# A fused attention, expert and gated kernel: the gated stage in blocks of 512 tokens, with the last 64 tokens of all batches as one unit

## The chip, the cores and the metric

One NeuronCore of a Trainium2 chip runs the whole kernel. The metric is the device time of one execution in microseconds (us). TensorE is clocked at one of two levels, 1.2 or 2.4 GHz; the profile gives the granted share of the upper one.

## The reference

Three layers follow each other. The first is an attention over 32 memory slots for each of 8 heads; the second gives each token one of 8 experts (two products with a ReLU between, scaled by a probability p); the third, the one that changes here, is a gated convolution along the tokens. S = 576 tokens, B = 4 batches, model width 512, inner width 1024:

```python
h = np.maximum(x @ w_in, 0.0)                     # [4, 576, 1024]
hp = zero-padded h, one token on each side
conv_out = sum(conv_w[k] * hp[:, k:k + 576] for k in range(3))
gate = 1.0 / (1.0 + np.exp(-conv_out))
out = (h * gate) @ w_out                          # [4, 576, 512]
```

Everything is float32. The kernel gets that precision from a faster type by writing each operand as a high and a low part and adding three products (high with high, high with low, low with high).

## The kernel before

The attention and the experts run batch by batch, with a product order written out by hand. An expert stage leaves its output `y` (not yet times p) in the DRAM buffer `ydram`, in 8 stores of 288 tokens for each batch, issued by GpSimd (POOL). The last product of batch 3 is followed on TensorE by the gated stage, the function `gated`, with no gap in the program.

The gated stage holds the inner dimension on the partitions, in 8 blocks of 128 (`f`), and tokens along the free axis. For each batch `b` it loads `y` and the row p (`load_y`, `load_p`), multiplies them and splits the product into `yh` and `yl` (`split_y`). Then, for each `f`:

- TensorE adds 12 terms (4 pieces of the model width, 3 products each) into the PSUM tile `pi`. A bank holds 512 float32 columns, so the 576 tokens stand as two halves of 288 in two banks (`banks`, two such pairs): 24 products of 288 columns.
- ScalarE (ACT) takes the ReLU out of PSUM into `ht` and multiplies by the middle tap into `ct`. VectorE (DVE) adds the two other taps (two operations), ScalarE takes the sigmoid, VectorE multiplies (`gm`), ScalarE and VectorE split the result into the tile `g` (`gs`; for f = 3, 4 and 6 the subtraction is GpSimd's). `ht` and `ct` come from one ring of 6 buffers (tag `cv`), so three blocks can be under way.
- GpSimd copies the last 64 tokens of `g` into `tail`, which holds two batches side by side.

After the 8 blocks, TensorE multiplies by `w_out` in chunks of 128 tokens (`po`, 24 products of 512 columns each): four chunks for each batch, and after an odd batch a fifth for the 64-token tails of two batches. That makes 18 chunks. The buffers of `y` (tag `ay`) are two in all, shared with the attention's last operand.

The order on TensorE is that of the program in the expert stage and in batch 0 of the columns (`tc.keep_in_program_order`); elsewhere a scheduler of the compiler lays the instructions of every engine in order when the program is built, and each engine then works its list strictly in that order, waiting on semaphores. SyncE (SP) issues the loads, in its own order.

```python
matmul3([(ps[:, hf, :HALF], half(hf)) for hf in range(2)],
        [((wi[kc][:, 0, fs], wi[kc][:, 1, fs]), (yh[:, kc, :], yl[:, kc, :])) for kc in range(4)],
        tc.keep_in_program_order if b == 0 else lambda ins: ins)
```

Of the kernel before, what the change touches and what calls it, by code (L numbers as in the profile page):

```python
# [24 lines left out]
HALF = S // 2  # L25
EPS = 1e-9
# [90 lines left out]
def fused_kernel(tc, q, first, first_q, kv, kv_tail, phi, w1, w2, w_in, conv_w, w_out, out):  # L117
# [3 lines left out]
    with (  # L121
# [779 lines left out]
        def load_p(name, e, b):  # L901

            p = late[1].tile([128, S], F32, tag="p", bufs=2, name=f"p{name}")
            nc.sync.dma_start(p, pdram[ds(e + 8 * b, 1), :].to_broadcast([128, S]))
# [16 lines left out]
        def y_parts(b):  # L921
            return [late[1].tile([128, 4, S], F32R, tag=t, bufs=1, name=f"{t}{b}") for t in ("yh", "yl")]
# [100 lines left out]
        def gated(gp, nm, scaled=False):  # L1023
# [9 lines left out]
            tail = None  # L1033
            for b in range(B):
                yh, yl = ys
                gs = []
                if b + 1 < B:
                    yn = load_y(b + 1, first(b + 1))
                if b % 2 == 0:
                    tail = gp.tile([128, 8, 2, 128], F32R, tag="tail", bufs=1, name=f"tail{b}")  # L1040
                to = 64 * (b % 2)
                def gate(f, ht, ct):
                    nc.scalar.activation(ct, ct, AF.Sigmoid)  # L1043
                    slow(f"gm.{f}").tensor_tensor(ct, ht, ct, ALU.mult)  # L1044
                    t = gp.tile([128, 2, S], F32R, tag="g", name=f"g{nm}{b}_{f}")

                    def finish():
                        split(t[:, 0, :], t[:, 1, :], ct, slow(f"gs.{f}"))
                        nc.gpsimd.tensor_copy(tail[:, f, :, to:to + 64], t[:, :, 512:576].bitcast(F32))  # L1049

                    gs.append(t)
                    return finish

                before = None
                for f in range(8):
                    fs = slice(f * 128, (f + 1) * 128)
                    ps = banks(f"pi{b}_{f}")
                    matmul3([(ps[:, hf, :HALF], half(hf)) for hf in range(2)],
                            [((wi[kc][:, 0, fs], wi[kc][:, 1, fs]), (yh[:, kc, :], yl[:, kc, :])) for kc in range(4)],
                            tc.keep_in_program_order if b == 0 else lambda ins: ins)  # L1060
                    finish = gate(*before) if before else lambda: None
                    ht = lp.tile([128, S], F32, tag="cv", name=f"ht{b}_{f}")
                    nc.scalar.activation(two(ht), halves(ps), AF.Relu)  # L1063
                    ct = lp.tile([128, S], F32, tag="cv", name=f"ct{b}_{f}")
                    nc.scalar.activation(ct, ht, AF.Copy, scale=convw[:, 1, f:f + 1])  # L1065
                    nc.vector.scalar_tensor_tensor(  # L1066
                        ct[:, 1:], ht[:, :S - 1], convw[:, 0, f:f + 1], ct[:, 1:], ALU.mult, ALU.add)
                    nc.vector.scalar_tensor_tensor(  # L1068
                        ct[:, :S - 1], ht[:, 1:], convw[:, 2, f:f + 1], ct[:, :S - 1], ALU.mult, ALU.add)
                    finish()  # L1070
                    before = f, ht, ct
                    while len(wo) < 4 and f >= WO[len(wo)]:
                        wo.append(w2_piece(f"wo{len(wo)}", slow(f"wo.{len(wo)}")))
                gate(*before)()
# [4 lines left out]
                def product(ps, c, fr, cols=slice(0, 512)):  # L1079
# [104 lines left out]
```

## Time and profile before

| | us |
|---|---|
| three timed runs | 411.52, 411.10, 409.93; median 411.1 |
| the profiled execution, its time | 411.57 |
| the profiled execution, its span | 409.8 |
| TensorE busy | 402.3 (98% of the span) |
| VectorE, ScalarE, GpSimd busy | 276.0, 221.8, 75.0 |

The span runs from the first to the last recorded instruction, so 1.8 us of the execution's time lie around it. Times in the rows are counted from the start of the span. The gated stage fills its second half, from 205.6 on. In a row, "x" is a count, and the square bracket tells how long the engine was idle before the row and who ended that. "PEld" is TensorE's weight load, which overlaps its products; busy times of overlapping products can't be added up.

### The profile page before, as it was taken

To read this page: it belongs to the slowest core of one execution; us is meant where nothing else is said; L and a number is where in the kernel's file an instruction comes from. 1 tells how busy PE (TensorE), PEld (TensorE's weight loads), DVE (VectorE), ACT (ScalarE), POOL (GpSimd) and SP (SyncE) were. 2 spreads that over 40 slices of the span, in tenths; PEclk is the share of its full clock that TensorE was granted. 3 is DMA by queue.
4 is the path that set the end of the run, shared out by engine and by line. 5 is a ranking of instruction groups with operands and counts; after the bars stand their busy time and mean duration, and the time that the engine had idled before them with its cause. 6 is when DMAs were issued, how large, how long until landed. Compare 5 with 4: busy or idle time off the path is not lost. (4 is left out here: it accounts for less than half of the span.)

```text
span 409.8 us, 8399 instructions
## 1 busy us (share of the span) xinstructions
PE 402.3 (98%) x3350; PEld 369.3 (90%) x3351; DVE 276.0 (67%) x505; ACT 221.8 (54%) x420; POOL 75.0 (18%) x125
## 2 busy tenths in 40 slices
PE   7999999999999999999999999999999999999996
PEld 6769989899998998999999988998889998999884
DVE  2689798897787986696879981679204793077700
ACT  4457567564566456465857652677215772267411
POOL 1000101402122211310101620033200233004400
PEclk9999999999999999999999999999999999999999
DMA  7999989999484959947550032000020000200022
GB/s 269 334 391 408 353 262 316 386 416 412 116 298 161 360 182 387 385 157 199 184 162 2 0 117 102 2 0 2 23 81 26 2 0 2 102 2 0 2 81 56
DMA packets 23888, 69.04 MB, mean 168 GB/s; under 512 B 3264, under 2 KB 4032, under 8 KB 23840
## 3 DMA queue, kind: packets, MB, share of 16 engines
q1 hardware_dynamic: 20256, 56.88, 39.2%
q0 software_dynamic: 3584, 11.54, 7.2%
q8 instruction: 28, 0.46, 0.5%
q14 instruction: 20, 0.16, 0.1%
HBM read 52.08 MB, written 16.33 MB: 167 GB/s over the span
## 5 line engine op out<-in xcount | busy, mean ns | idle before, releaser
L166 PE MATMUL py<-h,wb 128*128 128x288 f32 x768 | 105.3, 296 | 0.2 <-DVE h L807 0.2
L166 PEld LDWEIGHTS py<-h,wb 128*128 128x128 f32 x768 | 102.3, 188 | 1.2 <-issue 0.4
L166 PE MATMUL pi<-yh,wi 128*128 128x288 f32 x512 | 91.0, 296 | 0.0
L1084 PE MATMUL po<-wo,g 128*128 128x512 f32 x360 | 84.2, 389 | 0.0
L1084 PEld LDWEIGHTS po<-wo,g 128*128 128x128 f32 x360 | 67.0, 188 | 13.1
L166 PEld LDWEIGHTS pi<-yh,wi 128*128 128x128 f32 x512 | 76.6, 189 | 1.1 <-ACT ht L1063 0.2
L1066 DVE SCALAR_TENSOR_TENSOR ct<-ht,convw,ct 128x575 f32<-128x575 f32 x32 | 31.0, 968 | 51.2 <-ACT ct L1065 51.2
L166 PE MATMUL pi<-yl,wi 128*128 128x288 f32 x256 | 54.7, 295 | 0.0
L166 PE MATMUL ph<-att,vh 128*128 128x288 f32 x256 | 53.2, 301 | 0.2 <-DVE h L807 0.2
L1049 POOL CAST tail<-g 128x128 fp32r<-128x128 f32 x32 | 23.0, 722 | 123.2 <-DVE g L154 122.6
L891 POOL DMA_DIRECT2D ydram<-ys x32 | 17.6, 549 | 144.8 <-ACT ys L890 126.2
L166 PEld LDWEIGHTS ph<-att,vh 128*128 128x128 f32 x256 | 40.5, 188 | 3.7 <-DVE h L807 1.5
L166 PEld LDWEIGHTS pi<-yl,wi 128*128 128x128 f32 x256 | 41.1, 188 | 0.0
L1063 ACT ACTIVATE ht<-pi 128x576 f32<-128x576 f32 x32 | 20.8, 649 | 32.7 <-PE pi L166 32.7
L166 PE MATMUL ph<-att,vl 128*128 128x288 f32 x128 | 37.5, 294 | 0.0
L807 DVE SCALAR_TENSOR_TENSOR h<-ph,h 128x288 fp32r<-128x288 f32 x64 | 27.7, 449 | 12.1 <-ACT h L806 11.9
L806 ACT ACTIVATE h<-ph 128x288 fp32r<-128x288 f32 x64 | 25.4, 409 | 18.2 <-PE ph L166 18.0
L1110 ACT ACTIVATE ot<-po 128x512 f32<-128x512 f32 x17 | 9.5, 598 | 42.1 <-PE po L1084 42.1
L1044 DVE TENSOR_TENSOR ct<-ht,ct 128x576 f32<-128x576 f32 x32 | 27.0, 845 | 7.3 <-ACT ct L1043 7.1
L890 ACT ACTIVATE ys<-py 128x288 f32<-128x288 f32 x32 | 13.1, 408 | 33.9 <-issue 18.4
L153 ACT ACTIVATE g<-ct 128x576 fp32r<-128x576 f32 x32 | 21.7, 680 | 13.0 <-DVE ct L1044 13.0
L1068 DVE SCALAR_TENSOR_TENSOR ct<-ht,convw,ct 128x575 f32<-128x575 f32 x32 | 28.4, 886 | 0.4
(231 smaller groups left out, 513.0 us busy)
## 6 DMA issues: line engine op xcount, KB each, us to landing
kv<-in_kv SPq DMA_DIRECT2D x14, 512.0 KB, 8.3
q<-in_q SPq DMA_DIRECT2D x8, 576.0 KB, 10.1
ydram<-ys POOLq DMA_DIRECT2D x32, 144.0 KB, 5.3
y<-ydram SPq DMA_DIRECT2D x4, 1152.0 KB, 6.5
out<-ot SPq DMA_DIRECT2D x15, 256.0 KB, 2.1
ph<-in_phi SPq DMA_DIRECT2D x8, 288.0 KB, 7.4
adram<-at POOLq DMA_DIRECT2D x8, 288.0 KB, 7.2
wa_1r<-in_w SPq DMA_DIRECT2D x4, 512.0 KB, 5.5
```

The source lines that it names most:

```text
L153: pin(nc.scalar.activation(hi, src, AF.Copy))
L166: pin(nc.tensor.matmul(ps, st, mv[:, cols], start=i == 0, stop=i == len(terms) - 1))
L806: nc.scalar.activation(t[:, 0, :], ps, AF.Relu)
L807: low = nc.vector.scalar_tensor_tensor(t[:, 1, :], ps, 0.0, t[:, 0, :].bitcast(F32), ALU.max, ALU.subtract)
L890: nc.scalar.activation(yt, ps, AF.Copy)
L891: stored.append(nc.gpsimd.dma_start(ydram[b, d, :, half(hf)], yt).ins)
L1044: slow(f"gm.{f}").tensor_tensor(ct, ht, ct, ALU.mult)
L1049: nc.gpsimd.tensor_copy(tail[:, f, :, to:to + 64], t[:, :, 512:576].bitcast(F32))
L1063: nc.scalar.activation(two(ht), halves(ps), AF.Relu)
L1066: nc.vector.scalar_tensor_tensor(ct[:, 1:], ht[:, :S - 1], convw[:, 0, f:f + 1], ct[:, 1:], ALU.mult, ALU.add)
L1068: nc.vector.scalar_tensor_tensor(ct[:, :S - 1], ht[:, 1:], convw[:, 2, f:f + 1], ct[:, :S - 1], ALU.mult, ALU.add)
L1084: last_product[:] = [nc.tensor.matmul(ps[:, cols], st[sp], w[:, mp, f % 2, cols], start=f == 0 and i == 0, stop=f == 7 and i == 2).ins]
```

## The change

Each batch's first 512 tokens are one product of 512 columns for each term and block (`MT`), in a single bank; four such banks stand in a pool of their own. Of its 512 columns 511 outputs are finished there, since token 511's convolution needs token 512. The last 66 tokens of every batch (`TW`; 64 of them new, two as neighbours) are loaded, scaled and split together (`load_tails`, `split_tails`), and make one unit of 4 x 66 = 264 columns, worked once between batch 0 and the products by `w_out`. It gives the 64 tail tokens of all batches and token 511 (`edge`), which GpSimd copies into each `g` (`close_main`). So `pi` has 4 x 96 products of 512 columns and 96 of 264, where it had 768 of 288. The products by `w_out` keep their number and shape; for the last batch their order is now the written one. The loads of `y` bring 512 tokens; eight small loads bring the tails. The convolution for the middle tap moves into `taps`. Apart from that, the keys and values of units 4 to 6 of the attention are loaded by one DMA where it was two.

```diff
+MT, TW = 512, 66
...
-                if u < 2 * B - 1:
+                if u < 4:
                     for i in range(2):
...
-            nc.sync.dma_start(y, ydram[b].rearrange("d p s -> p d s"))
-            return y, load_p(b, e, b) if e is not None else None
+            nc.sync.dma_start(y[:, :, :MT], ydram[b].rearrange("d p s -> p d s")[:, :, :MT])
+            return y[:, :, :MT], load_p(b, e, b, MT)[:, :MT] if e is not None else None
...
+        def load_tails(scaled):
+
+            y = state.tile([128, 4, S], F32, tag="ay", name="yt")[:, :, :B * TW]
+            p = None if scaled else late[1].tile([128, S], F32, tag="p", bufs=2, name="pt")[:, :B * TW]
+            for b in range(B):
+                if not scaled:
+                    nc.sync.dma_start(by_batch(p)[:, b], pdram[ds(expert(b) + 8 * b, 1), S - TW:].to_broadcast([128, TW]))
+                nc.sync.dma_start(y[:, :, TW * b:TW * b + TW], ydram[b].rearrange("d p s -> p d s")[:, :, S - TW:])
+            return y, p
+
+        def split_tails(yp, nm):
+            y, p = yp
+            t = state.tile([128, 2, 4, B * TW], F32R, tag="ay", name=f"ts{nm}")
+            parts = [t[:, i] for i in range(2)]
+            if p is not None:
+                nc.vector.tensor_tensor(y, y, p.rearrange("p (o s) -> p o s", o=1).to_broadcast([128, 4, B * TW]), ALU.mult)
+            split(*parts, y)
+            return parts
...
+            def taps(ct, ht, f, n, first):
+
+                w = lambda k: convw[:, k, f:f + 1]
+                more = min(n, ht.shape[-1] - first - 1)
+                nc.scalar.activation(ct, ht[..., first:first + n], AF.Copy, scale=w(1))
+                a = 1 - first
+                nc.vector.scalar_tensor_tensor(ct[..., a:], ht[..., :n - a], w(0), ct[..., a:], ALU.mult, ALU.add)
+                nc.vector.scalar_tensor_tensor(ct[..., :more], ht[..., first + 1:first + 1 + more], w(2), ct[..., :more],
+                                               ALU.mult, ALU.add)
+
+            def columns(name, y, store, pin=lambda ins: ins, between=lambda f: None):
...
-                    ps = banks(f"pi{b}_{f}")
-                    matmul3([(ps[:, hf, :HALF], half(hf)) for hf in range(2)],
...
+                    ps = pairs[-1].tile([128, 512], F32, tag="pi", bufs=1 if scaled else 4, name=f"pi{name}_{f}")[:, :n]
+                    matmul3([(ps, slice(0, n))],
+                            [((wi[kc][:, 0, fs], wi[kc][:, 1, fs]), (yh[:, kc, :], yl[:, kc, :])) for kc in range(4)], pin)
...
+            def store_tail(f, ct):
+                hi, lo = (by_batch(tail[:, f, i]) for i in range(2))
+                split(hi, lo, ct[:, :, 1:], slow(f"gs.{f}"))
+                split(edge[:, f, 0], edge[:, f, 1], ct[:, :, 0])
...
+                def close_main(f):
+                    nc.gpsimd.tensor_copy(gs[f][:, :, MT - 1:], edge[:, f, :, b:b + 1].bitcast(F32))
...
+                columns(f"{nm}{b}", ys, store_main, tc.keep_in_program_order if b == 0 else lambda ins: ins, between)
+                if b == 0:
+                    tails = split_tails(tails, nm)
+                    yn = load_y(1, first(1))
+                    columns(f"{nm}t", tails, store_tail)
+                    for f in range(8):
+                        close_main(f)
...
+                pin = tc.keep_in_program_order if b == B - 1 else lambda ins: ins
...
+        ps2_cm.__exit__(None, None, None)
+        pi_cm = tc.tile_pool(name="ps3", bufs=4, space=PSUM)
```

On TensorE, at the end of batch 0's columns (the number after `pi0_` is the block f; a row is a run of equal instructions). Before, the last block and then `po`:

```order
L166 MATMUL pi0_7_3346<-yh0_2931,wi3_2976 128x288 x2
L166 MATMUL pi0_7_3346<-yl0_2932,wi3_2976 128x288 x2
L166 MATMUL pi0_7_3346<-yh0_2931,wi3_2976 128x288 x2
L1084 MATMUL po0_0_3403<-wo0_3186,g0_1_3168 128x512 x2
L1084 MATMUL po0_0_3403<-wo1_3263,g0_2_3216 128x512 x3
```

Now the tails' blocks `pit` stand there, the first three ahead of any product by `w_out`:

```order
L168 MATMUL pi0_7_3264<-yh0_2928,wi3_2973 128x512
L168 MATMUL pi0_7_3264<-yl0_2929,wi3_2973 128x512
L168 MATMUL pi0_7_3264<-yh0_2928,wi3_2973 128x512
L168 MATMUL pit_0_3301<-ts_3293,wi0_2814 128x264 x3
...
L168 MATMUL pit_2_3345<-ts_3293,wi0_2814 128x264 x3
L168 MATMUL pit_2_3345<-ts_3293,wi1_2817 128x264 x3
L168 MATMUL pit_2_3345<-ts_3293,wi2_2970 128x264 x3
L168 MATMUL pit_2_3345<-ts_3293,wi3_2973 128x264 x3
L1146 MATMUL po0_0_3523<-wo0_3156,g0_0_3121 128x512 x3
```

The 24 products of a block became 12, and `pit_0` to `pit_2` come before the first `po`; the other five stand among `po`'s.

On VectorE, at the first convolutions of batch 0 (`ct0_1` is batch 0, block 1). Before, `y2`'s product with p stands ahead of them:

```order
L154 TENSOR_TENSOR wo3_3343<-wo3r_3184,wo3_3343 128x1024
L918 TENSOR_TENSOR y2_3515<-y2_3515,p2_3517 128x576 x4
L1066 SCALAR_TENSOR_TENSOR ct0_0_3100<-ht0_0_3098,convw_96,ct0_0_3100 128x575
L1068 SCALAR_TENSOR_TENSOR ct0_0_3100<-ht0_0_3098,convw_96,ct0_0_3100 128x575
L1066 SCALAR_TENSOR_TENSOR ct0_1_3134<-ht0_1_3132,convw_96,ct0_1_3134 128x575
```

Now the tails (`yt` times `pt`, then the low part `ts`) stand behind the first convolution, and `y1` times p stands 13 rows later:

```order
L156 TENSOR_TENSOR wo3_3261<-wo3r_3154,wo3_3261 128x1024
L1067 SCALAR_TENSOR_TENSOR ct0_0_3095<-ht0_0_3094,convw_96,ct0_0_3095 128x510
L933 TENSOR_TENSOR yt_3071<-yt_3071,pt_3072 128x4x264
L1068 SCALAR_TENSOR_TENSOR ct0_0_3095<-ht0_0_3094,convw_96,ct0_0_3095 128x511
L1067 SCALAR_TENSOR_TENSOR ct0_1_3116<-ht0_1_3115,convw_96,ct0_1_3116 128x510
L1068 SCALAR_TENSOR_TENSOR ct0_1_3116<-ht0_1_3115,convw_96,ct0_1_3116 128x511
L156 TENSOR_TENSOR ts_3293<-yt_3071,ts_3293 128x1056
...
L1067 SCALAR_TENSOR_TENSOR ct0_3_3175<-ht0_3_3174,convw_96,ct0_3_3175 128x510
L1098 TENSOR_TENSOR ct0_2_3140<-ht0_2_3139,ct0_2_3140 128x511
L942 TENSOR_TENSOR y1_3297<-y1_3297,p1_3299 128x512 x4
L1068 SCALAR_TENSOR_TENSOR ct0_3_3175<-ht0_3_3174,convw_96,ct0_3_3175 128x511
L1067 SCALAR_TENSOR_TENSOR ct0_4_3199<-ht0_4_3198,convw_96,ct0_4_3199 128x510
```

What moved: where VectorE's list held the load of `y2`, it now holds first the tails and then `y1`, whose load takes the buffer of `yt` and so waits for `ts`. Between `ts` and `y1` stand eight operations, and behind `y1` the multiplication of block 3 that frees a buffer of the ring.

## Rows read from the trace of the kernel before

**Rows 1.** The page: engines' busy time, and the granted clock in 40 slices.

```profile
PE 402.3 (98%) x3350; PEld 369.3 (90%) x3351; DVE 276.0 (67%) x505; ACT 221.8 (54%) x420; POOL 75.0 (18%) x125
...
PEclk9999999999999999999999999999999999999999
```

**Rows 2.** TensorE's waits over the run: releaser, total us, times, longest.

```profile
PE idle L477 <- POOL ident masks.py:199: 1.5, 1, 1.5
...
PE py L166 <- DVE h L807: 0.2, 1, 0.2
```

**Rows 3.** Busy time by stretch: gated batches 0 to 3, us and counts.

```profile
205.60:253.20 47.60, 47.60 (x291) 43.65 (x290) 38.10 (x46) 27.18 (x42) 11.60 (x12) 1.00 0.22 72
253.20:305.90 52.70, 52.70 (x314) 48.03 (x313) 26.18 (x33) 25.45 (x41) 10.14 (x11) 1.00 0.08 26
305.90:353.20 47.30, 47.30 (x290) 43.57 (x289) 26.18 (x33) 24.85 (x40) 10.13 (x11) 1.00 0.06 23
353.20:406.10 52.90, 52.85 (x313) 47.84 (x311) 23.68 (x29) 23.50 (x37) 9.47 (x11) 1.00 0.08 27
```

**Rows 4.** Timeline of TensorE: an unbroken run of `w_out` products.

```profile
232.32 18.07 PE L1084 MATMUL po<-wo,g 128*128 128x512 f32 x79
```

**Rows 5.** Groups by shape, 205 to 400: busy us, mean ns.

```profile
L1066 DVE SCALAR_TENSOR_TENSOR ct<-ht,convw,ct 128x575 f32<-128x575 f32 x32 | 31.0, 968 | 51.2 <-ACT ct L1065 51.2
L1068 DVE SCALAR_TENSOR_TENSOR ct<-ht,convw,ct 128x575 f32<-128x575 f32 x32 | 28.4, 886 | 0.4
...
L1049 POOL CAST tail<-g 128x128 fp32r<-128x128 f32 x32 | 23.0, 722 | 123.2 <-DVE g L154 122.6
...
L1063 ACT ACTIVATE ht<-pi 128x576 f32<-128x576 f32 x32 | 20.8, 649 | 32.7 <-PE pi L166 32.7
L154 POOL TENSOR_TENSOR g<-ct,g 128x576 fp32r<-128x576 f32 x12 | 17.9, 1492 | 17.3 <-ACT g L153 17.3
```

**Rows 6.** SyncE's issues of keys and values, and their first reader.

```profile
35.90 1.76 SPq L351 DMA_DIRECT2D kv<-in_kv  x2
...
kv<-in_kv SPq DMA_DIRECT2D x1, 1024.0 KB, 13.3
...
L427 PE MATMUL pk<-kv,a x64: 272/273/297, 58.6 to 60.8; 128*32 128x128 f32 x64
```

**Rows 7.** Timeline of GpSimd: the last three stores of `y`.

```profile
201.30 0.54 POOL L891 DMA_DIRECT2D ydram<-ys  x1 [3.74 <-ACT ys L890]
203.41 0.54 POOL L891 DMA_DIRECT2D ydram<-ys  x1 [1.57 <-ACT ys L890]
206.59 0.54 POOL L891 DMA_DIRECT2D ydram<-ys  x1 [2.63 <-ACT ys L890]
```

**Rows 8.** Time to landing: the stores issued at 201.30 and 206.59, one alone each.

```profile
DMA to landing us min/median/max: 2.0/2.0/2.0
...
DMA to landing us min/median/max: 6.7/6.7/6.7
```

**Rows 9.** Time to landing: loads of `y` (all four), and a small store.

```profile
DMA to landing us min/median/max: 5.4/6.5/7.8
...
out<-ot SPq DMA_DIRECT2D x6, 128.0 KB, 2.3
```

**Rows 10.** Timeline of VectorE at the start of the gated stage.

```profile
209.43 1.22 DVE L154 TENSOR_TENSOR wo<-wo3r,wo 128x1024 fp32r<-128x1024 f32 x1
212.92 2.77 DVE L918 TENSOR_TENSOR y<-y,p 128x576 f32<-128x576 f32 x4 [2.27 <-issue]
215.60 0.81 DVE L1066 SCALAR_TENSOR_TENSOR ct<-ht,convw,ct 128x575 f32<-128x575 f32 x1
...
229.69 1.88 DVE L1068 SCALAR_TENSOR_TENSOR ct<-ht,convw,ct 128x575 f32<-128x575 f32 x1
```

**Rows 11.** Timeline of GpSimd: two subtractions of `gs`.

```profile
229.46 3.42 POOL L154 TENSOR_TENSOR g<-ct,g 128x576 fp32r<-128x576 f32 x2 [1.28 <-ACT g L153]
```

**Rows 12.** Timeline of SyncE: the load of `y2`, issued with `y3`'s.

```profile
205.00 34.30 SPq L910 DMA_DIRECT2D y<-ydram  x2
```

More of the change, by code (lines that the diff above doesn't have):

```diff
@@ L1032, in gated @@
                 split_y(0, load_y(0, None), *ys)
[L1033 to L1052, printed above, removed]
+            tail = gp.tile([128, 8, 2, 256], F32R, tag="tail", bufs=1, name=f"tail{nm}")
+            edge = gp.tile([128, 8, 2, B], F32R, tag="edge", bufs=1, name=f"edge{nm}")
+            def taps(ct, ht, f, n, first):
[7 more added lines that the diff above has]
+            def columns(name, y, store, pin=lambda ins: ins, between=lambda f: None):
+                yh, yl = y
+                n = yh.shape[-1]
                 before = None
@@ L1063, in gated @@
[L1063 to L1069, printed above, removed]
@@ L1070, in gated @@
-                    finish()
-                    before = f, ht, ct
+                    ps = pairs[-1].tile([128, 512], F32, tag="pi", bufs=1 if scaled else 4, name=f"pi{name}_{f}")[:, :n]
+                    matmul3([(ps, slice(0, n))],
+                            [((wi[kc][:, 0, fs], wi[kc][:, 1, fs]), (yh[:, kc, :], yl[:, kc, :])) for kc in range(4)], pin)
+                    finish = gate(*before, store) if before else lambda: None
+                    ht = lp.tile([128, S], F32, tag="cv", name=f"ht{name}_{f}")[:, :n]
@@ new lines, in columns, with gate @@
+                    before = f, own, ct
+                    between(f)
+                gate(*before, store)()
+            def gate(f, own, ct, store):
+                nc.scalar.activation(ct, ct, AF.Sigmoid)
+                slow(f"gm.{f}").tensor_tensor(ct, own, ct, ALU.mult)
+                return lambda: store(f, ct)
+            def store_tail(f, ct):
+                hi, lo = (by_batch(tail[:, f, i]) for i in range(2))
+                split(hi, lo, ct[:, :, 1:], slow(f"gs.{f}"))
+                split(edge[:, f, 0], edge[:, f, 1], ct[:, :, 0])
@@ new lines, in gated, with store_main, between @@
+            for b in range(B):
+                gs = []
+                if b == 0:
+                    tails = load_tails(scaled)
+                elif b + 1 < B:
+                    yn = load_y(b + 1, first(b + 1))
+                def store_main(f, ct):
+                    t = gp.tile([128, 2, MT], F32R, tag="g", name=f"g{nm}{b}_{f}")
+                    split(t[:, 0, :MT - 1], t[:, 1, :MT - 1], ct, slow(f"gs.{f}"))
+                    gs.append(t)
+                    if b:
+                        close_main(f)
+                def close_main(f):
+                    nc.gpsimd.tensor_copy(gs[f][:, :, MT - 1:], edge[:, f, :, b:b + 1].bitcast(F32))
+                def between(f):
@@ L1077, in gated, with product @@
                     split_y(b + 1, yn, *ys)
-                def product(ps, c, fr, cols=slice(0, 512)):
+                pin = tc.keep_in_program_order if b == B - 1 else lambda ins: ins
+                def product(ps, c, fr):
                     for f in fr:
                         w = wo[f // 2].rearrange("p s (i d) -> p s i d", i=2)
-                        st = [gs[f][:, s, c * 128:(c + 1) * 128] if c < 4 else tail[:, f, s, :] for s in range(2)]
+                        to = slice(64 * (b - 1), 64 * (b + 1))
+                        st = [gs[f][:, s, c * 128:(c + 1) * 128] if c < 4 else tail[:, f, s, to] for s in range(2)]
                         for i, (sp, mp) in enumerate(((0, 0), (0, 1), (1, 0))):
-                            last_product[:] = [nc.tensor.matmul(ps[:, cols], st[sp], w[:, mp, f % 2, cols],
-                                                                start=f == 0 and i == 0, stop=f == 7 and i == 2).ins]
+                            last_product[:] = [pin(nc.tensor.matmul(ps, st[sp], w[:, mp, f % 2, :],
+                                                                    start=f == 0 and i == 0, stop=f == 7 and i == 2)).ins]
                 chunks = [0, 1, 2] + [4] * (b % 2) + [3]
```

28 lines of the change are left out of this document (18 added, 10 removed).

## The prediction

> **What bounds the kernel now.** I read the page first: TensorE is busy 402.3 of 409.8 us and its granted clock is 1.00 in every slice, the level of 2.4 GHz [rows 1]. The list of TensorE's waits has seven rows of 3.3 us in all, from 1.5 down to 0.2 us each, and none on a line of the gated stage [rows 2]. So a microsecond less of TensorE work there is a microsecond less in all, as long as nothing new makes TensorE wait. The stretches of the four gated batches say the same: 47.60, 52.70, 47.30 and 52.85 us busy of as much, while VectorE is busy 38.1, 26.2, 26.2 and 23.7 us and ScalarE less than 28 in each [rows 3]. VectorE is near full in the first batch alone, so that is where to look for new waits.
>
> **What a product costs.** 79 products of 512 columns take 18.07 us [rows 4]; the last one's own 389 ns off, 78 steps are 17.68 us, 226.7 ns each. The third gated batch holds 192 products of 288 columns and 96 of 512 (4 chunks of 24) in 47.30 us [rows 3]: 47.30 - 96 x 0.2267 = 25.54 us, over 192 that is 133.0 ns. 288 columns at 2.4 GHz are 120.0 ns and 512 are 213.3, so each product costs some 13 ns beside its columns, of either length.
>
> The Trainium skill has a much smaller number for this: "TensorE: Matmul & The Clock Gate", in the section on 56 against 53.3 ns, gives a fixed cost of about 2.5 ns for each matmul of a warm stream. By it, 288 products fewer would save 0.7 us and the 768 columns more would take back 0.3: a change of 0.4 us, an estimate from that page. The rows show 13 ns here, so they decide.
>
> **The change part by part, on TensorE.** Before: 768 x 133.0 ns = 102.1 us. After: 4 batches x 96 = 384 products of 512 columns at 226.7 ns = 87.1 us, and 96 of 264 columns. None of 264 is in the trace. A line through the two known lengths (93.7 ns for 224 columns, 0.418 ns each) gives 123.0 ns, and no less than that is reason to expect; the nearest row, 288 columns, gives 133.0 as the upper bound. So 11.8 us (12.8 at the upper bound). The sum is 98.9 us, 3.2 less than before (2.2 at the upper bound). I take 123.0, since the step from 288 to 264 columns is small and the cost beside the columns was equal at both known lengths. The products by `w_out` stay 432 of 512 columns, and the expert stage stays.
>
> **On the other engines.** Everything per block shrinks with its columns: 4 x 512 + 264 = 2312 columns instead of 2304 for each f, in 5 units instead of 4. VectorE's two tap operations had means of 968 and 886 ns, with 0.81 for one alone [rows 5, 10]; the tails add 8 units of about half that. The gain there is GpSimd's 32 copies of 722 ns [rows 5], which are replaced by 32 copies of two elements per partition. ScalarE's ReLU, 649 ns for 576 columns [rows 5], now covers 512. From the second batch on these engines are half idle [rows 3] and the work hides under TensorE: a block takes 12 x 226.7 ns = 2.72 us there; VectorE's two tap operations and two multiplications or subtractions, 0.81 and 0.69 us each at 576 columns [rows 10], about 2.7 at 511; and the 96 or 120 products by `w_out` (21.8 or 27.2 us) leave it time to catch up. Without that cover the held-up means of [rows 5] (0.1 us more for each tap operation) would cost 0.2 us a block, 1.6 a batch.
>
> The merged loads of keys and values cost nothing that I can see: units 4's were issued at 35.9 and first read at 58.6, 22.7 us later, and the one load that was already 1024 KB landed 13.3 us after its issue [rows 6]. The expert order's end, the branch and the last two copies are the same.
>
> **The one new chain.** The tails of batch 3 are the last thing that the expert stage stores. VectorE now has them at the second place of its convolutions, and `y1`'s load waits until they are split. Let T be the time at which VectorE starts `yt` times p.
>
> - The last store is issued at 206.59 [rows 7]. It landed 6.7 us later, while the one issued at 201.30 took 2.0 [rows 8]. The difference has a neighbour: the load of `y2`, 1152 KB, issued at 205.00 [rows 12]. The change moves that load away, so I take 2.0, landing at 208.6, and keep 6.7 (213.3) as the other bound.
> - The tail's load, 135 KB in 512 runs: a 128 KB transfer takes 2.3 us, a whole `y` in 512 runs 5.4 at best [rows 9]. I take 3.0, near the one of its size, and 0.4 for the issue. T = 208.6 + 0.4 + 3.0 = 212.0; bounds 211.3 and 219.1.
> - From T, VectorE does `yt` (1056 elements; 1.2 us as for 1024 in [rows 10]), three tap operations of 0.7 and the split, 1.2 (0.81 and, for a multiplication, 2.77 / 4 at 576 columns [rows 10], cut to 511: 0.7 and 0.6): `y1`'s load is issued at T + 4.5. It takes L: 5.4 to 7.8 us [rows 9], 6.0 taken for 1024 KB without a neighbour.
> - Three tap operations and five of 0.6 later, at T + 9.6, VectorE reaches `y1` times p, and it stands there until T + 4.5 + L. Then four products of 0.6, three tap operations and two of 0.6 end with block 3's multiplication, which frees the ring buffer that block 6's ReLU needs; with 0.6 for that ReLU its bank is free at T + 10.8 + L.
> - `pit_2` takes that bank. TensorE reaches it at 205.6 + 96 x 0.2267 + 24 x 0.123 = 230.3.
>
> With T = 212.0 and L = 6.0 the bank is free at 228.8, 1.5 us early: the chain is hidden. Each microsecond by which T + L passes 219.5 costs TensorE one.
>
> **The sum.** -3.2 us of TensorE, and I lay 0.2 us for short waits in the first batch: 411.57 - 3.0 = 408.6 on the scale of the profiled execution. That execution is 0.5 above the median of the runs; from 411.1 I get **408.1 us**.
>
> **The rivals.**
>
> *VectorE runs out in the first batch.* It was busy 38.1 of 47.6 us there and now gets the eight tail units, some 11 us, and the tails' scaling and split, while `y1`'s scaling comes in and `y3`'s can wait. While GpSimd subtracts, VectorE is held up: an operation of 0.81 us took 1.88 beside 3.42 us of it [rows 10, 11]. Three such blocks and three tail units of half the length lie in that stretch of about 55 us. If each holds VectorE for 1.1 us the later `pit` blocks wait 1 to 4 us in all; the time is 409.1 to 412. For it speaks how full VectorE is; against it, that GpSimd's copies, 23 us over the stage, go away.
>
> *Transfers as slow as they now are at this place: the slower end.* If the store lands at 213.3 whatever loads beside it, the tail takes 5.4 and `y1` 7.8, then T = 219.1, T + L = 226.9, and `pit_2` waits 7.4 us: 411.1 - 3.2 + 7.4 = 415.3. It decides for slower by over 0.5% from T + L = 224.8 on (5.3 us of waiting). Against it stands that the moved load is the only large one at that place. The Trainium skill, "DMA: Bandwidth & Descriptors", section on specifications, says that a transfer under 512 B is below line rate; the tail's runs are 264 B. No row here shows a load of such runs alone, so that sentence moves no bound.
>
> *The change saves nothing: time goes by columns alone.* If a product of 512 columns cost here what 288 cost, by length (133.0 x 512/288 = 236.4 ns), the stage would be 384 x 236.4 ns + 96 x 121.9 = 102.5 us, and the time 411.5. The fixed cost in that page of the skill is so small that it comes near this. Against it speak 18 chunks of products of that very length at 226.7.
>
> **How the numbers follow.** About 0.5% (2.1 us) is what a measurement of this kernel can tell from no change. I give the forecast 0.60 (its own range 407.2 to 409.0), VectorE running out 0.20, slow transfers 0.13, no saving 0.07. Faster by over 0.5% is below 409.0: the forecast, 0.60. Within 0.5%: rival one and rival three, 0.27. Slower: 0.13. The range goes from 407.0 to 411.6: it takes in the upper bound of the 264 columns, most of the first rival and the third, and leaves out the slow transfers.
>
> **What would show it.** Right: blocks of `pi` 2.72 us apart, no wait of TensorE on a `pi` line, the last store landing near 208.6, VectorE at `yt` near 212, TensorE's last product some 3 us earlier. The first rival would show as waits of TensorE at `pit` blocks for a ReLU, with VectorE full before them; the second as one long wait at `pit_2` or ahead of it, with VectorE idle at `yt` or `y1`; the third as steps of 236 ns. I would be wrong altogether if a wait came in a later batch, where I see nothing that could make one, or if the merged loads delayed the attention.

## The result, and the profile after

The changed kernel takes **407.57 us** (median of six runs, 406.41 to 407.89); the kernel before took 411.02 in runs beside them. The ratio is 0.9916, 95% interval 0.9900 to 0.9933. The forecast was 408.1, with a range of 407.0 to 411.6.

The profiled execution's span is 405.7 us, 4.1 less than before. The list of TensorE's waits, with the releaser, total, times and longest, has six rows, all in the attention and the expert stage:

```profile
PE idle L479 <- POOL ident masks.py:199: 1.5, 1, 1.5
...
PE pk L429 <- DMA kv<-in_kv: 0.6, 2, 0.4
...
PE pk L419 <- DMA kt<-in_kv_tail: 0.2, 1, 0.2
```

None is on a line of the gated stage, as before [rows 2]. Busy time of the four gated batches, in the columns of [rows 3]: the stretch and its length, then busy time and number of instructions of TensorE, its weight load, VectorE, ScalarE and GpSimd, then the granted clock, the DMA engines' busy share and GB/s. The first stretch now holds the tails of all batches:

```profile
204.88:260.23 55.35, 55.35 (x290) 47.71 (x289) 48.70 (x86) 38.19 (x83) 12.28 (x20) 1.00 0.27 87
260.23:309.24 49.01, 49.01 (x217) 40.55 (x216) 24.39 (x33) 23.84 (x41) 6.72 (x11) 1.00 0.09 28
309.24:352.82 43.58, 43.58 (x194) 36.04 (x192) 24.38 (x33) 23.24 (x40) 6.72 (x11) 1.00 0.07 25
352.82:401.99 49.17, 49.17 (x217) 40.36 (x215) 21.99 (x29) 21.98 (x37) 5.78 (x6) 1.00 0.09 29
```

TensorE is busy in all of each stretch. The four are 197.11 us together, where those of [rows 3] were 200.50: **3.4 us less**. The third holds 96 products of `pi` and 96 by `w_out`; 43.58 - 96 x 0.2267 = 21.82 us, over 96 that is 227.3 ns. The tails stand in TensorE's timeline in two runs of three blocks and one of two:

```profile
226.67 4.54 PE L168 MATMUL pit<-ts,wi 128*128 128x264 f32 x36
231.05 5.19 PE L1146 MATMUL po<-wo,g 128*128 128x512 f32 x22
```

36 products of 264 columns lie between 226.67 and 231.05: 121.7 ns each. The rest of the span's 4.1 us is at the start: the first gated product comes at 204.88, 0.7 earlier than before, though TensorE's work ahead of it is the same (the first experiment is on that). So 0.7 us of the 4.1 did not come from the gated stage.

The new chain in the timelines of GpSimd, SyncE and VectorE (start, duration, engine):

```profile
205.83 0.54 POOL L893 DMA_DIRECT2D ydram<-ys  x1 [2.63 <-ACT ys L892]
...
208.02 0.36 SPq L925 DMA_DIRECT2D yt<-ydram  x1
...
210.49 1.26 DVE L933 TENSOR_TENSOR yt<-yt,pt 128x1056 f32<-128x1056 f32 x1 [0.52 <-DMA yt<-ydram]
...
215.06 0.36 SPq L912 DMA_DIRECT2D y<-ydram  x1
...
220.27 2.50 DVE L942 TENSOR_TENSOR y<-y,p 128x512 f32<-128x512 f32 x4
```

The issues of that stretch, each with its size and the time to landing:

```profile
y<-ydram SPq DMA_DIRECT2D x1, 1024.0 KB, 5.1
...
ydram<-ys POOLq DMA_DIRECT2D x1, 144.0 KB, 2.0
yt<-ydram SPq DMA_DIRECT2D x1, 132.0 KB, 2.3
```

The last store lands after 2.0 us where it took 6.7 [rows 8]; the tail's load follows it and lands 2.3 us after its issue. So T is 210.49, L is 5.1, and VectorE finds `y1` there when it gets to it: the load lands at 220.2 and VectorE starts on `y1` at 220.27, so its own operations and the load end together. Block 6's ReLU, which empties the bank that `pit_2` takes, stands in ScalarE's timeline:

```profile
226.52 0.58 ACT L1084 ACTIVATE ht<-pi 128x512 f32<-128x512 f32 x1
```

It ends at 227.1, and TensorE reaches `pit_2` at 229.58, 2.5 us later. From T + L = 215.6 the chain could by this trace come 2.5 us later, to 218.1.

On VectorE and GpSimd, groups by shape between 200 and 402 us (answering [rows 5]):

```profile
L1068 DVE SCALAR_TENSOR_TENSOR ct<-ht,convw,ct 128x511 f32<-128x511 f32 x32 | 30.5, 953 | 0.5
...
L1067 DVE SCALAR_TENSOR_TENSOR ct<-ht,convw,ct 128x510 f32<-128x510 f32 x32 | 23.9, 748 | 46.7 <-ACT ct L1065 46.7
...
L1121 POOL CAST g<-edge 128x2 fp32r<-128x2 f32 x32 | 12.1, 392 | 38.1 <-PE po L1146 27.6 <-DVE edge L156 10.2
```

GpSimd's 32 copies went from 722 ns to 392 each.

### The profile page after: what moved, and what is told of

The parts are those of the page before. It is cut to its first block, busy times and chain, and to the rows that moved or that the text cites. A ratio compares the mean times of both kernels' runs of the same rounds, so it can differ in the third digit from the quotient of the medians.

```text
span 405.7 us, 7947 instructions
## 1 busy us (share of the span) xinstructions
PE 398.0 (98%) x3062; PEld 350.0 (86%) x3063; DVE 281.7 (69%) x544; ACT 227.6 (56%) x461; POOL 65.2 (16%) x128
## 5 line engine op out<-in xcount | busy, mean ns | idle before, releaser
L168 PE MATMUL pi<-yh,wi 128*128 128x512 f32 x256 | 79.6, 390 | 0.0
L168 PEld LDWEIGHTS pi<-yh,wi 128*128 128x128 f32 x256 | 48.1, 188 | 10.0
L1067 DVE SCALAR_TENSOR_TENSOR ct<-ht,convw,ct 128x510 f32<-128x510 f32 x32 | 23.9, 748 | 46.7 <-ACT ct L1065 46.7
L168 PE MATMUL pi<-yl,wi 128*128 128x512 f32 x128 | 49.8, 389 | 0.0
L156 POOL TENSOR_TENSOR g<-ct,g 128x511 fp32r<-128x511 f32 x12 | 16.5, 1372 | 104.5 <-ACT g L155 103.1
L1068 DVE SCALAR_TENSOR_TENSOR ct<-ht,convw,ct 128x511 f32<-128x511 f32 x32 | 30.5, 953 | 0.5
L1084 ACT ACTIVATE ht<-pi 128x512 f32<-128x512 f32 x32 | 19.0, 594 | 20.7 <-PE pi L168 20.7
L168 PEld LDWEIGHTS pi<-yl,wi 128*128 128x128 f32 x128 | 24.0, 188 | 5.0
L155 ACT ACTIVATE g<-ct 128x511 fp32r<-128x511 f32 x32 | 19.7, 625 | 13.7 <-DVE ct L1098 13.3
L1098 DVE TENSOR_TENSOR ct<-ht,ct 128x511 f32<-128x511 f32 x32 | 23.5, 736 | 5.3 <-ACT ct L1097 5.0
```

The lines of the kernel that those rows point to most:

```text
L155: pin(nc.scalar.activation(hi, src, AF.Copy))
L156: pin((eng or nc.vector).tensor_tensor(lo, src, hi.bitcast(F32), ALU.subtract))
L168: pin(nc.tensor.matmul(ps, st, mv[:, cols], start=i == 0, stop=i == len(terms) - 1))
L1067: nc.vector.scalar_tensor_tensor(ct[..., a:], ht[..., :n - a], w(0), ct[..., a:], ALU.mult, ALU.add)
L1068: nc.vector.scalar_tensor_tensor(ct[..., :more], ht[..., first + 1:first + 1 + more], w(2), ct[..., :more], ALU.mult, ALU.add)
L1084: nc.scalar.activation(ht, ps, AF.Relu)
```

## The experiments

In TensorE's lists `pi` with a first number are the batches' blocks, `pit` the tails'. Where an experiment adds work, its product is read by nothing or changes no value.

**1. The loads of keys and values apart again.**

```diff
-                if u < 4:
+                if u < 2 * B - 1:
```

> The changed kernel with the loads of keys and values of units 4 to 6 as two DMAs again; the rest as changed. Theory: the merged loads are hidden (22.7 us lay between issue and first read before), so the time stays at 407.6 within 0.25 us, and the first gated product starts within 0.1 us of 204.8. Rival: the merge gave the 0.5 us or so by which the changed kernel reaches the gated stage earlier than the kernel before; then this one is at 408.1 and its first gated product at 205.4.

Measured: 408.08 us, ratio to before 0.9930 (0.9914 to 0.9946). The interval overlaps the changed kernel's, but the time is the one that I gave for the rival, so the trace has to decide. In the profiled execution the first gated product comes at 205.84, 0.96 later than in the changed kernel; but so much was lost already at the first keys, which both kernels load in the same way. The first `pk` products, with their wait in the bracket, in the changed kernel and here:

```profile
7.35 0.64 PE L429 MATMUL pk<-kv,a 128*32 128x128 f32 x16 [0.44 <-DMA kv<-in_kv]
```

```profile
8.53 0.64 PE L429 MATMUL pk<-kv,a 128*32 128x128 f32 x16 [1.60 <-DMA kv<-in_kv]
```

1.18 us of difference at 7.4, before any load that the edit touches is read. The other traces say the same. Over all profiled executions of this document the gated stage begins between 204.45 and 205.84. From the first `pk` product to it pass 197.3 to 197.8 us in the four that load keys and values apart, and 197.0 to 198.2 in the ten with merged loads. The kernel before, as varied in experiments 3 and 4, loads them apart and reaches the stage at 204.91 and 204.67, as early as the changed kernel. So the merged loads gave nothing that these runs show, and how early the gated stage begins varies by over a microsecond from one execution to another, mostly with the start of the first `pk`. The wait for the first keys makes the difference between the two rows above; in the kernel before, whose first `pk` came at 7.82, TensorE waited 0.19 us there, for ScalarE. What remains is the stage's own 3.4 us.

**2. The last batch's products in the scheduler's order.**

```diff
-                pin = tc.keep_in_program_order if b == B - 1 else lambda ins: ins
+                pin = lambda ins: ins
```

> The changed kernel with the last batch's products by w_out left to the scheduler's order; the rest as changed. Theory: it moves two runs of products by a few places and every operand is there by then, so the time stays at 407.6 within 0.2 us. Rival: the written order saves a wait for the last block's g; then a wait of 0.3 to 1 us appears on a po line of the last batch and the time is up to 408.6.

Measured: 407.55 us, ratio 0.9921 (0.9904 to 0.9938), and no wait of TensorE in the gated stage. The written order gives nothing that this run shows.

**3. The kernel before, cut as 512 and 64.**

```diff
-                    matmul3([(ps[:, hf, :HALF], half(hf)) for hf in range(2)],
+                    matmul3([(ps[:, 0, :512], slice(0, 512)), (ps[:, 1, :64], slice(512, 576))],
...
-                    nc.scalar.activation(two(ht), halves(ps), AF.Relu)
+                    nc.scalar.activation(ht[:, :512], ps[:, 0, :512], AF.Relu)
+                    nc.scalar.activation(ht[:, 512:], ps[:, 1, :64], AF.Relu)
```

> The kernel before with its 576 tokens cut as 512 and 64 columns in two banks where they stood as 288 and 288: same number of products, same columns, two ReLUs for one. If each product costs its columns and a constant 13 ns, a pair takes 226.7 + 39.5 = 266.2 ns, as two of 288 do (266.0), and the time stays at 411. If there is a floor under a short product, near TensorE's mean weight load (369.3 us over 3351, 110 ns), a pair takes some 337 ns and the time rises by 384 x 71 ns = 27 us to 438. If long products are cheaper than the constant says, so that the gain of the change came from their length, the time falls below 410.

Measured: 439.64 us, ratio 1.0703 (1.0680 to 1.0725). The floor is there, and the second ReLU is not the reason: TensorE's list has no wait on a `pi` line. The second gated batch:

```profile
259.61:319.71 60.10, 60.10 (x313) 51.26 (x312) 28.20 (x33) 26.61 (x49) 9.98 (x11) 1.00 0.07 23
```

60.10 less 120 products by `w_out` (27.2) leaves 32.9 for 96 pairs, 342.7 ns each; less 226.7 for the long one, 116 ns for 64 columns.

**4. Four lengths in one run** (the kernel before; 288 + 288, 320 + 256, 384 + 192 and 448 + 128 in batches 0 to 3).

```diff
+                    cut = (288, 320, 384, 448)[b]
-                    matmul3([(ps[:, hf, :HALF], half(hf)) for hf in range(2)],
+                    matmul3([(ps[:, 0, :cut], slice(0, cut)), (ps[:, 1, :576 - cut], slice(cut, 576))],
...
```

> The kernel before with another cut of the 576 tokens in each batch, 288 + 288, 320 + 256, 384 + 192 and 448 + 128 in batches 0 to 3 (two ReLUs for one); products and columns are the same in number. If a product costs its columns at 2.4 GHz and 13 ns, but never less than the 115 ns that 64 columns took, a pair takes 266, 267, 289 and 315 ns, the blocks (12 pairs) are 3.2, 3.2, 3.5 and 3.8 us apart, and the time is 96 x (1 + 23 + 49 ns) = 7 us above before, 418. If only very short products are dear and the constant of 13 ns holds down to 128 columns, all blocks are 3.2 us apart and the time is 411.

Measured: 417.18 us, ratio 1.0166 (1.0135 to 1.0198): the floor's 418, not 411.

```profile
252.15:304.98 52.83, 52.83 (x314) 48.10 (x312) 26.19 (x33) 25.93 (x49) 10.16 (x11) 1.00 0.08 26
304.98:354.08 49.10, 49.10 (x290) 45.32 (x288) 28.47 (x33) 25.91 (x48) 8.38 (x11) 1.00 0.06 22
354.08:411.56 57.48, 57.48 (x313) 51.07 (x311) 25.85 (x29) 24.54 (x45) 8.44 (x11) 1.00 0.08 25
```

By the same subtraction (120, 96 and 120 products by `w_out`) a pair takes 267.0, 284.8 and 315.4 ns. The long product at its columns and 13.3 ns, about what 288 and 512 columns take beside theirs (146.6, 173.3 and 200.0), leaves 120 ns for 256 columns, which is columns and 13; 111 for 192, where that would be 93; and 115 for 128, where it would be 67. So down to 256 columns a product costs its columns and 13 ns, and at 192, 128 and 64 it costs 111, 115 and 116: **a product does not get cheaper below some 235 columns**, the length at which columns and 13 ns come to 111 (worked out; none between 192 and 256 was run). The tails' 264 columns are just above.

The Trainium skill, "TensorE: Matmul & The Clock Gate", section "LDWEIGHTS (loading the stationary operand)", gives a weight load as its columns divided by 1.2, in ns: 106.7 for 128 columns, an estimate from that page, and says under "Back-to-back issue gap" that the spacing is set by both operations. These runs agree within 10 ns. The figure of about 131 ns for 512 columns that stands there does not hold for this stream, where they take 226.7. That the floor is the weight load is argued: the loads had 128 columns in every run.

**5. Two banks for the gated blocks,** first with the order left to the compiler's scheduler, then with the changed kernel's order.

```diff
-                    ps = pairs[-1].tile([128, 512], F32, tag="pi", bufs=1 if scaled else 4, name=f"pi{name}_{f}")[:, :n]
+                    ps = pairs[-1].tile([128, 512], F32, tag="pi", bufs=1 if scaled else 2, name=f"pi{name}_{f}")[:, :n]
...
-        pi_cm = tc.tile_pool(name="ps3", bufs=4, space=PSUM)
+        pi_cm = tc.tile_pool(name="ps3", bufs=2, space=PSUM)
```

> The changed kernel with two banks for the gated blocks where it has four. A block then takes the bank of the block two before it. From the trace of the changed kernel: block 6's ReLU ends at 227.1 where pit_0 is reached at 226.7, block 7's at 231.3 where pit_1 is reached at 228.1, so pit_0 waits 0.4 us and pit_1 about 2.8 in all, pit_2 then waits for pit_0's ReLU. Theory (the waits that the changed kernel escapes in the first batch are those of banks): TensorE waits 3 to 5 us at pit blocks of the first batch and nothing in later batches, time 410.6 to 412.6. Rival (two banks are enough, since the ring of ht and ct limits the blocks anyway): within 0.5 us of 407.6. The step of an unhindered block stays 2.72 us by both.

Measured: 408.52 us, ratio 0.9947 (0.9925 to 0.9968), no wait of TensorE on a `pi` or `pit` line. My theory missed: it took the order for given. The scheduler had put runs of `po` ahead of and between the blocks from `pi0_5` on, and `pit_0` came at 231.2 where it was at 226.7.

So the order was held: at the end of the program each instruction of TensorE, VectorE and ScalarE is tied behind the one ahead of it in the changed kernel's lists (`lists` holds them as positions).

```diff
+        for eng, runs_ in lists.items():
+            traced = [i for i in nc.cur_bb.bb.instructions if i.engine == eng]
+            wanted = [traced[k + j] for k, n in runs_ for j in range(n)]
...
+            for a, z in zip(wanted, wanted[1:]):
+                tc.add_manual_dep(z, a.name, mybir.DependencyInfo(mybir.DependencyClass.NoSync, mybir.DependencyReason.DATA), reason="order")
```

> The changed kernel with two banks for the gated blocks where it has four, in the order of the changed kernel on all engines. Theory (from the trace of the changed kernel: block 6's ReLU ends 0.4 us after TensorE reaches pit_0, block 7's 3.2 us after it reaches pit_1, and pit_2 then waits for pit_0's ReLU): TensorE waits 3 to 5 us at pit blocks of the first batch and nothing later, time 410.6 to 412.6. Rival (two banks are enough in this order too): no wait over 0.5 us, time within 0.7 of 407.6.

Measured: 413.46 us, ratio 1.0060 (1.0043 to 1.0077). TensorE's timeline has four waits, 4.7 us, all at `pit` blocks:

```profile
227.21 1.73 PE L168 MATMUL pit<-ts,wi 128*128 128x264 f32 x12 [0.31 <-ACT ht L1084]
231.42 1.74 PE L168 MATMUL pit<-ts,wi 128*128 128x264 f32 x12 [2.48 <-ACT ht L1084]
234.73 1.74 PE L168 MATMUL pit<-ts,wi 128*128 128x264 f32 x12 [1.57 <-ACT htt L1084]
...
244.98 1.73 PE L168 MATMUL pit<-ts,wi 128*128 128x264 f32 x12 [0.32 <-ACT htt L1084]
```

The first three are where the trace of the changed kernel said, and about as long (0.4 and 2.8 us, then `pit_0`'s ReLU); a fourth follows at `pit_5`. The time is 0.9 above the upper end of what I gave: from its first to its last product the stage is 6.0 us longer for 4.7 of listed waits. Part of the rest fits the overlap that each wait breaks (a product of 264 columns lasts 284 ns where the step is 121.7); that was not tested. Four banks are worth 5.9 us in this order. In the order that the scheduler makes for two they are worth 1.0, hardly clear of noise: the interval of that ratio overlaps the changed kernel's. Holding the order costs nothing by itself as far as the traces show: from the first product of batch 1 to the first of the last chunk TensorE takes 136.16 us in the changed kernel and in this run, and as much within 0.01 us in the held run of experiment 6 and in the last one of experiment 7. No run held the order and changed nothing else.

**6. More work on VectorE in the first batch,** with a free order (in place, and ScalarE's middle tap waits for it), then with the changed kernel's order (into a spare tile; the loop of experiment 5 is added).

```diff
+                    if name == "0":
+                        nc.vector.tensor_tensor(ht, ht, ht, ALU.max)
```

> The changed kernel with one more operation on VectorE for each of batch 0's eight blocks, the maximum of ht with itself (512 columns, about 0.6 us, which changes no value): 4.8 us more of VectorE's work before the tails' blocks. Theory (VectorE had little room in the first batch, the smallest margin in the trace being 1.1 us at pit_5): TensorE waits 3 to 4.5 us at pit blocks, time 410.6 to 412. Rival (VectorE has room and catches up while TensorE works at the first chunks of po): no wait above 0.5 us, time within 0.5 of 407.6.

Measured: 408.39 us, ratio 0.9935 (0.9909 to 0.9962), no wait in the gated stage: here again the scheduler moved the blocks (`pit_5` came at 247.6, in the changed kernel at 239.0).

```diff
+                    if name == "0":
+                        spare = lp.tile([128, S], F32, tag="spare", bufs=1, name=f"spare{f}")[:, :n]
+                        nc.vector.tensor_tensor(spare, ht, ht, ALU.max)
```

> The changed kernel with eight more operations on VectorE in the first batch (the maximum of ht with itself into a spare tile that nothing reads, one just ahead of each block's first convolution operation, some 0.65 us each, 5.2 us in all), and with the order of TensorE, VectorE and ScalarE held to the changed kernel's own, where the run with more VectorE work before had let the compiler's scheduler lay a new one. Theory (the margins read from the trace hold for the order as it stands: 2.5 us at pit_2, 1.1 at pit_5): TensorE waits 3 to 4.5 us at pit blocks, time 410.6 to 412.1. Rival (VectorE had that much room in any order): no wait over 0.5 us, time 407.6 within 0.5.

Measured: 411.95 us, ratio 1.0037 (1.0023 to 1.0051). The eight operations took 0.68 us each, 5.5 in all; TensorE waits at `pit_4` and `pit_5`, as the smallest margin said, somewhat less than I gave:

```profile
238.59 1.72 PE L168 MATMUL pit<-ts,wi 128*128 128x264 f32 x12 [0.27 <-ACT htt L1084]
242.37 1.74 PE L168 MATMUL pit<-ts,wi 128*128 128x264 f32 x12 [2.07 <-ACT htt L1084]
```

The median is 4.4 us above the changed kernel's; the profiled execution, the fastest of the five, is 3.6 above, of which 0.6 is a later start of the stage and 2.9 the stage itself.

**7. A large transfer beside the last store.** The first one, with a free order:

```diff
+        other = dram.tile([3, 128, S], F32, name="other")
...
+                if not scaled and b == B - 1:
+                    nc.sync.dma_start(other, ydram[b, :3])
```

> The changed kernel with one more DMA, 864 KB from the buffer of y into a scratch buffer in DRAM, issued by SyncE just ahead of the last store of y (at about 205.5); it adds work that nothing reads, and takes the place that y2's load had in the kernel before. Theory (the neighbour made the last store land after 6.7 us and its absence makes it 2.1): the store lands 5 to 7 us after its issue, at 211 to 213, VectorE starts the tails at T = 214 to 216.5 where it is 210.5 in the changed kernel, T + L is 219 to 222 where it is 215.6, and beyond 218.1 each microsecond costs TensorE one at pit_2 or the blocks next to it: time 408.5 to 411.5. Rival (the slow landing belonged to the place, not to the neighbour, and went for another reason): the store lands after 2 to 3 us, T = 210.5 to 211.5, time 407.6.

Measured: 407.90 us, ratio 0.9929 (0.9907 to 0.9950). The neighbour does hold the store up, by 2.7 us where [rows 8] had 4.7:

```profile
other<-ydram SPq DMA_DIRECT2D x1, 864.0 KB, 5.3
...
ydram<-ys POOLq DMA_DIRECT2D x1, 144.0 KB, 4.7
```

T was 213.47, just under the range I gave, and TensorE waited for nothing. This does not test the margin, since VectorE's order was a new one here too (two tap operations ahead of `yt` instead of one, and two operations between `yt` and `ts` instead of three): block 6's ReLU ended at 228.3, 1.2 us later than in the changed kernel for a T that was 3.0 later, and 1.6 before TensorE reached `pit_2`.

Then 2592 KB, in the held order (the loop of experiment 5 added) and in a free one:

```diff
-        other = dram.tile([3, 128, S], F32, name="other")
+        other = dram.tile([3, 3, 128, S], F32, name="other")
...
-                    nc.sync.dma_start(other, ydram[b, :3])
+                    nc.sync.dma_start(other, ydram[1:, :3])
```

> The changed kernel with one more DMA of 2592 KB from the buffer of y into a scratch buffer in DRAM, issued by SyncE just ahead of the last store of y; nothing reads it; the order of TensorE, VectorE and ScalarE is held to the changed kernel's. Theory (slow transfers cost TensorE one for one beyond T + L = 218.1): with 864 KB the store landed after 4.7 us where it took 2.1 alone, so with three times that after 8 to 11, at 214 to 217; T = 217 to 220, T + L = 222 to 227, TensorE waits 4 to 9 us at pit blocks, time 411.5 to 416.5. Rival (the chain is hidden even then, or the store isn't held up more than by 864 KB): T under 214, no wait over 0.5 us, time 407.6 to 408.1.

> The same DMA of 2592 KB, with the compiler's scheduler free to lay a new order: it puts the tails' operations on VectorE some ten places later and spreads the pit blocks among the products by w_out. Theory (a slow chain costs what the order makes it cost, and a new order hides most of it): the same late store and T as with the held order, but TensorE waits under 1.5 us, time 407.6 to 409.2. Rival (the chain itself is too long for any order): the wait is the held order's within 1 us.

Measured: 438.32 us, ratio 1.0659 (1.0631 to 1.0688), in the held order, and 431.93, ratio 1.0504 (1.0483 to 1.0525), in the free one. Both expectations missed by far, in the size of the delay. The store landed after 10.6 us, as I gave, but the tail's load behind it took 24.9 us for 132 KB:

```profile
ydram<-ys POOLq DMA_DIRECT2D x1, 144.0 KB, 10.6
yt<-ydram SPq DMA_DIRECT2D x1, 132.0 KB, 24.9
```

VectorE stood at `yt` until T = 242.3, and TensorE waited 25.0 us in one piece at `pi0_6`, ahead of `pit_2`, since the ring of `ht` and `ct` had stopped:

```profile
242.32 1.26 DVE L936 TENSOR_TENSOR yt<-yt,pt 128x1056 f32<-128x1056 f32 x1 [31.61 <-DMA yt<-ydram]
```

```profile
247.18 0.79 PE L168 MATMUL pi<-yh,wi 128*128 128x512 f32 x1 [25.05 <-ACT ht L1087]
```

With two short ones at `pit` blocks its waits are 27.3 us in all; T + L - 218.1 is 29.2 (L is 5.0 here). In the free order it waited 19.1 us at `pit_0`: with so late a T the order that the scheduler laid hid little of the chain, and my theory for that run was wrong.

Why so slow: while TensorE stood still and hardly anything else moved, the DMA engines' mean busy share (the number before the last) was 0.20, some three of 16:

```profile
222.20:226.00 3.80, 0.00 (x0) 0.00 (x0) 0.00 (x0) 0.00 (x0) 0.00 (x0) 1.00 0.20 87
```

The Trainium skill, "DMA: Bandwidth & Descriptors", section "Why a DMA increments its semaphore by 16 and not by 1", under "How many engines (k)", says that a transfer runs on the largest number of engines, up to 16, that divides the slowest dimension of both its sides. That is 3 here, and the share agrees (0.18 over 228.0 to 247.1). The 864 KB have 3 as their first dimension in the program as well, and landed after 5.3 us; they lie in one piece on both sides, and that they were therefore spread over more engines is argued, as it is that the tail's load waited for its packets on those three.

The price itself needed a delay between the two; in the held order:

```diff
+        more = dram.tile([4, 128, S], F32, name="more")
...
+                    near = nc.sync.dma_start(other, ydram[b, :3]).ins
+                    with tc.issue_after(near):
+                        nc.sync.dma_start(more, ydram[b - 1])
```

> The changed kernel in its own order on TensorE, VectorE and ScalarE, with two DMAs beside the last store of y: the 864 KB of the earlier run, which landed after 5.3 us, and 1152 KB more right behind it, from the buffer of y into scratch buffers in DRAM that nothing reads. Theory (a late chain costs TensorE one for one beyond T + L = 218.1): at the rate of the 864 KB both take some 12 us, to 217.5; the store lands 6 to 11 us after its issue and T = 215 to 220, L some 5 us, T + L = 220 to 225, and TensorE waits 2 to 7 us, T + L - 218.1 within 1 us: time 409.5 to 415. Rival (the price is not one for one: the order has other margins, or a wait spreads): TensorE waits less than half of T + L - 218.1 or more than twice as much.

Measured: 413.23 us, ratio 1.0054 (1.0027 to 1.0081). The timelines of VectorE and TensorE:

```profile
215.79 1.26 DVE L939 TENSOR_TENSOR yt<-yt,pt 128x1056 f32<-128x1056 f32 x1 [6.15 <-DMA yt<-ydram]
...
227.79 1.61 PE L168 MATMUL pit<-ts,wi 128*128 128x264 f32 x12
232.44 2.94 PE L168 MATMUL pit<-ts,wi 128*128 128x264 f32 x12 [3.03 <-ACT ht L1090]
```

The issues of that stretch with size and time to landing:

```profile
more<-ydram SPq DMA_DIRECT2D x1, 1152.0 KB, 7.8
y<-ydram SPq DMA_DIRECT2D x1, 1024.0 KB, 5.1
...
ydram<-ys POOLq DMA_DIRECT2D x1, 144.0 KB, 7.6
```

T + L = 215.8 + 5.1 = 220.9, 2.8 beyond 218.1, and TensorE waits 3.0 us, once, at `pit_2`. One for one, at the place that the prediction named. (L is as in the changed kernel, and VectorE again gets to `y1` as its load lands, so what this run moved is T; what a longer L alone would do was not tried.) But the block after the wait takes 2.94 us where the one before takes 1.61, the 22 products by `w_out` behind it take 5.57 where they took 5.19, and the stage is 4.9 us longer for 3.0 of waiting. The granted clock (the third number from the end) of the stretches behind the wait:

```profile
229.24:232.44 3.20, 0.17 (x3) 0.01 (x1) 3.20 (x7) 2.51 (x6) 0.46 (x1) 1.00 0.21 78
...
233.00:235.50 2.50, 2.50 (x12) 2.50 (x12) 2.50 (x4) 2.50 (x6) 1.09 (x2) 0.50 0.00 0
...
236.50:240.00 3.50, 3.50 (x17) 2.88 (x16) 3.50 (x6) 1.81 (x5) 0.06 (x1) 1.00 0.28 58
```

TensorE ran at the level of 1.2 GHz for some three microseconds after it had been idle for 3.0. The 1.3 and 0.4 us that those products lost are nearly all of the difference between 4.9 and 3.0. After the 25.0 us of waiting with the 2592 KB it did the same:

```profile
247.20:251.00 3.80, 3.80 (x9) 3.03 (x10) 3.58 (x7) 3.80 (x8) 0.00 (x0) 0.50 0.78 248
```

## Why the prediction was right, point by point

- **TensorE's sum.** Right in size and in kind. 512 columns were put at 226.7 ns and took 227.3, 264 were put at 123.0 and took 121.7. The sum said 3.2 us less, the stage shows 3.4. The reason given, 13 ns beside the columns for every product, held only where it was used: experiments 3 and 4 show that it ends at a floor of 111 to 116 ns. The line through two lengths was carried to 264 columns without a look at what lies below, and that the floor begins just under 264 was luck. Narrower tail units (two batches each, 132 columns) would have been sized at 68 ns a product, 13 us for 192 of them, and would have taken some 22 at the 115 ns of 128 columns: an estimate from these runs.
- **The rival "no saving"**, by which time goes by columns alone, is out: steps of 227 ns, not 236. With it goes the 2.5 ns of the Trainium skill ("TensorE: Matmul & The Clock Gate", section "Wait — 56ns, not 53.3ns?") as a price for this stream, which would have made a change of 0.4 us.
- **The chain.** Right. The store's landing was put at 2.0 us without its neighbour and took 2.0; T came at 210.5 instead of 212.0, since the store itself was 0.8 earlier and the tail's load took 2.3 and not 3.0; L was 5.1 and not 6.0. The margin at `pit_2` was put at 1.5 us and is 2.5. T + L came 2.4 us earlier than put, but TensorE got there 0.7 earlier too, and the bank came free 0.7 later than the prediction's T + 10.8 + L gives from the measured T and L (226.4): ScalarE had an operation of its own ahead of block 6's ReLU, which the chain left out. That the neighbour made the store slow is shown: with 864 KB beside it 4.7 us, with both transfers 7.6.
- **The rival "slow transfers".** It did not come, and its mechanism was right: beyond the margin the wait is one for one, and at `pit_2` or ahead of it. Its price was too low, since it took no account of the clock: 3.0 us of waiting cost 4.9 (experiment 7).
- **The rival "VectorE runs out".** It did not come, though VectorE is busy 48.70 of 55.35 us in the first batch. The margin in this order is real and small: 5.5 us more work brought 2.3 us of waits. In an order laid for that work there is none (experiment 6). What I missed is that the scheduler decides how much room VectorE has; the sum of busy time did not.
- **Short waits** in the first batch, put at 0.2 us: none. **The merged loads**, put at nothing, and **the written order**, not priced: nothing, as far as two runs tell.
- **The scale.** The median of before was 411.1 in the forecast and 411.02 beside the changed kernel; the change is 3.45 us where I gave 3.0. The forecast was 0.5 too high: 0.2 are the short waits that did not come, 0.2 the stage's larger gain, and 0.1 the median of before.

## What to carry to other kernels

Fewer, longer products save their fixed share only above the length at which a product stops getting cheaper; find that length from a run with two or three lengths before sizing a remainder unit. A margin read from a trace belongs to the order of that trace: an experiment that tests it must hold the order, or the compiler's scheduler can hide what is to be measured. And a wait of TensorE can cost more than its length, since the clock may fall behind it.

## What was not expected of the hardware

- The clock after a wait: 3.0 us of idleness were followed by a granted clock of 0.50 for about 3 us (experiment 7); after the wait of 2.5 us in experiment 5 the profiled execution still shows 1.00 in each stretch (its mean clock is 0.999; that of the three other runs is 0.996). In experiment 6 with the held order the five runs had mean clocks from 0.995 to 1.000, and the times go with them: 412.82 and 412.65 at 0.995, 411.14 at 1.000.
- A product of 64 columns takes 116 ns in this stream and one of 264 takes 121.7.
- A transfer of 2592 KB from DRAM to DRAM, shaped with 3 as its slowest dimension, kept the busy share near 0.20 of 16 engines, and a load of 132 KB issued while it ran landed after 24.9 us instead of 2.3.
- `pk`'s wait for the first keys was 0.4 us in one execution and 1.6 in another, and the gated stage began 0.96 us apart.
